# A state-space scan with an MLP behind it: another order of transfers and first steps in the opening

## The chip, the cores and the metric

The kernel runs on one core of a Trainium2 chip. The metric is the device time of one execution in microseconds (us), as the median of the runs shown. Five engines work side by side, each through its own instructions in order: PE (TensorE, the matrix products), VectorE (DVE), ScalarE (ACT), GpSimd (POOL) and SyncE (SP). DMA transfers are issued here from two queues, SP's and ACT's. Tiles in SBUF hold operands, banks of PSUM hold the results of products.

## The reference

Two blocks, one behind the other. The first is a Mamba-2 style scan over 4 batches and 8 heads of 768 positions, with heads of 32 and a state of 16; the second is an MLP with a hard swish over the 3072 resulting rows of 256.

```python
log_a = np.log(np.clip(a, 1e-06, 1.0))
for c in range(nc):                                   # chunks along the sequence
    cum = np.cumsum(la, axis=-1)
    L = np.exp(cum[:, :, :, None] - cum[:, :, None, :]) * causal
    M = np.einsum('bhin,bhjn->bhij', Cc, Bc) * L
    y_intra = np.einsum('bhij,bhjd->bhid', M, xc)
    y_inter = np.einsum('bhin,bhnd->bhid', Cc, state) * np.exp(cum)[:, :, :, None]
    y[:, :, sl] = y_intra + y_inter
    state = decay_full * state + sum_j(B_j x_j * decay_from_j)
h = y_rows @ w_in                                     # (3072, 256) @ (256, 2048)
g = h * np.clip(h + 3.0, 0.0, 6.0) / 6.0
out = g @ w_out                                       # (3072, 2048) @ (2048, 256)
```

Activations are float32; the weights come as 64-bit floats, read as pairs of 32-bit words.

## The kernel before, in words

The sequence is cut into 6 chunks of 128 positions (the kernel's `c` and `k`), each with two halves of 64. A chunk of all 4 batches gives 512 rows for the MLP. While PE multiplies chunk k's MLP, the other engines prepare the scan of the chunk behind it. The program order is written out by hand: each engine runs its instructions in the order in which the code names them, so a waiting instruction holds up what is behind it on its engine. Transfers wait in the same way on the queue that issues them.

**Inputs of chunk 0.** `a` (96 KB), B (`tokens_first`, 256 KB in runs of 64 bytes), C (`pairs_first`, eight transfers of 32 KB, one for each batch and parity of head, in runs of 256 bytes), x (512 KB in runs of 128 bytes), and the weights, eight pieces of 1 MB (`load_w`, rows of 4 KB for `w_in` and 2 KB for `w_out`), of which three fit into SBUF at a time (`raw`). Pieces 0 to 3 are `w_in`, 4 to 7 `w_out`.

**Decoding a piece of weights** (`decode(i)`, advanced by `weights(i, n)` in n steps). 1: ACT copies the upper 16 bits (L198); for piece 0 VectorE also builds the significand (L201, L205). 2: VectorE takes exponent and sign (L215, L217), and L201 for the other pieces. 3: ACT, L221. 4: ACT, L223, with VectorE's L205 for the other pieces; then the piece three further on is loaded. 5: VectorE, L228 and L236, which writes the finished float32 weights to `w_in[i]` or `w_out`.

**The scan of chunk 0.** VectorE clips and adds up log a (L264, L269) and splits the sums (`in_three`); PE forms differences in four banks f0 to f3 (`diff`), ACT their exponentials L (`diff_exp`, L365), and `first_eto` the decay from the chunk's start (L376). `turn_b` turns B on PE (L422) and copies it on ACT (L431). `turn_squares` transposes C on VectorE (L465) and `part_heads` splits it by head parity (L475). `scores` multiplies C and B on PE (L530); `into_state` multiplies B, faded by POOL (`ends`, L396), with x (L544). `multiply` has ACT copy the states (`take` L560, `mid` L569) and VectorE multiply the scores into L (L574). `mix` multiplies that with x (L600) and the state with C (`from_state`, L503); `keep` copies the result to `yT` on ACT (L614). `renew` (L583, L554) forms the next state on VectorE. Also there: `add_up` of the later chunks' sums with `store_rows`, two transfers to DRAM (L286, L288), `turn_cum` (four transposes on PE, L316) with `by_token` (L319), differences and exponentials of chunk 1, and `busy(n, bank)`, n products of the identity with itself that nobody reads (L493).

**The MLP of chunk 0.** 16 groups of products `mlp_in` (L622) over the four banks f0 to f3, each followed by `ramp` on ACT (L726) and `times_ramp` on VectorE (L731), which frees the bank; the decoding of pieces 2 to 5 is woven in between. Group f needs `w_in[f // 4]`. Then `first_out` (L744) multiplies with `w_out`, the first quarter of it first.

The order of the opening ends with the first weights' fifth step, `turn_cum`, chunk 1's share of decoding (piece 1), `mix(0)`, `keep(0)`, and transfers for chunk 1.

Of the kernel before, what the change touches and what calls it, by code (L numbers as in the profile page):

```python
# [8 lines left out]
FP32 = mybir.dt.float32  # L9
# [12 lines left out]
def kernel(  # L22
# [24 lines left out]
    nc = tc.nc  # L47
    P = 128
    NB, NH, S, D = x.shape
    N = B.shape[-1]  # L50
    DM, DF = moe_w_in.shape[0], moe_w_out.shape[0]
    NC = S // P
# [23 lines left out]
    G = NB * NH  # L76
# [9 lines left out]
    def load_bc(c):  # L86

        sl = slice(c * P, (c + 1) * P)  # L90

        def tokens_first(src, queue=nc.sync, **where):
            t = loads.tile([P, NB * NH, N], FP32, **where)
            queue.dma_start(out=t, in_=src[:, :, sl, :].rearrange("b h s n -> s (b h) n"))
            return t

        def pairs_first(src):
            t = loads.tile([P, 2, NB, 4, N], FP32, name="pairs", tag="bc")
            for b in range(NB):
                for h in range(2):  # L100
                    nc.sync.dma_start(  # L101
                        out=t[:, h, b].rearrange("s a n -> s (a n)"),
                        in_=src[b, h:NH:2, sl, :].rearrange("h (s a) n -> h s (a n)", a=4))
            return t

        if 0 < c < TURN:
            bcs[c] = [tokens_first(C, name="C", tag="bc")]
        Bs[c] = tokens_first(B, nc.scalar if c == 0 else nc.sync, name="B", bufs=1)
        if c == 0:
            bcs[c] = [pairs_first(C), Bs[c]]  # L110
        elif c < TURN:
            bcs[c].append(Bs[c])
        else:
            bcs[c] = [pairs_first(C), pairs_first(B)]

    def load_x(c):
        sl = slice(c * P, (c + 1) * P)
        xts[c] = loads.tile([P, NB * NH, D], FP32, name="xt", bufs=1)
        nc.sync.dma_start(out=xts[c], in_=x[:, :, sl, :].rearrange("b h s d -> s (b h) d"))
# [5 lines left out]
    NRAW = 3  # L125
    raws = {}

    def load_w(i, queue=nc.sync):

        raw = loads.tile([P, NK * FP * 2 * P], U32, name="raw", bufs=NRAW)  # L130
        if i < NP:
            cols = slice(2 * i * FP * P, 2 * (i + 1) * FP * P)
            src = moe_w_in[:, cols].rearrange("(k p) f -> p k f", p=P)
            dst = raw.rearrange("p (k f) -> p k f", k=NK)
        else:
            r0 = (i - NP) * FP * P
            src = moe_w_out[r0:r0 + FP * P, :].rearrange("(k p) m -> p k m", p=P)
            dst = raw.rearrange("p (k m) -> p k m", k=FP)
        queue.dma_start(out=dst, in_=src)
        raws[i] = raw  # L140

    load_w(0, nc.scalar)
    load_bc(0)
    load_x(0)
    load_w(1)
    nc.scalar.preload_act_table_set("natural_log_exp_and_others")


# [119 lines left out]
    def add_up(sl):  # L268
        nc.vector.tensor_tensor_scan(  # L269
            out=cum[:, sl], data0=run.rearrange("g c p -> g (c p)")[:, sl], data1=a_sb[:, sl],  # L270
            initial=0.0, op0=ALU.mult, op1=ALU.add)
# [13 lines left out]
    def store_rows():  # L285
        nc.sync.dma_start(  # L286
            out=cum_e[1:].rearrange("c g p -> g c p"), in_=cum_c[:, 1:])
        nc.sync.dma_start(  # L288
            out=cum_d[2:].rearrange("c a g i -> g (c a) i"),
            in_=cum[:, 2 * P:].rearrange("g (k i) -> g k i", i=HT))  # L290
# [23 lines left out]
    def turn_cum(c_ps):  # L314
        for c in range(2, NC):
            nc.tensor.transpose(out=c_ps[:, c], in_=cum_c[:, c], identity=ident[:G, :G])  # L316
# [45 lines left out]
    def diff_exp(c, b):  # L362
        if c not in Ls:
            new_decays(c)
        nc.scalar.activation(Ls[c][:, b], ds.pop((c, b)), AF.Exp)  # L365

    def first_eto():

        e_ps = ps.tile([P, NB, HT], FP32, name="e_ps", tag="f0")
        for b in range(NB):  # L370
            nc.tensor.matmul(
                out=e_ps[:, b],
                lhsT=picks[:, b * P:(b + 1) * P],
                rhs=split[:, 0, HALF[1]], start=(b == 0), stop=True, skip_group_check=True)
        etos[0] = att.tile([P, NB, P], FP32, name="eto")
        nc.scalar.activation(etos[0][:, :, HALF[1]], e_ps, AF.Exp)  # L376
# [30 lines left out]
    def turned(c):  # L407
        if c not in bTs:
            bTs[c] = [att.tile([P, NB, P], FP32, name="bT", bufs=1),
                      att.tile([P, NB, 2, P], FP32, name="cT", bufs=1),  # L410
                      att.tile([P, NB, P], FP32, name="csT", bufs=1)]
        return bTs[c]
# [14 lines left out]
    def turn_b(c):  # L427

        t_ps = turn_ps(c, 1)
        transposes(c, 1, t_ps)  # L430
        nc.scalar.copy(out=turned(c)[0], in_=t_ps)  # L431
# [31 lines left out]
    def turn_squares(t, out):  # L463

        nc.vector.transpose(  # L465
            out=out.rearrange("r b (s a) -> r b a s", a=4),
            in_=t.rearrange("s t b a n -> s (b a) t n"))

    def part_heads(c):
        _, cT, csT = turned(c)  # L470
        for t in range(2):
            if c == TURN:
                nc.scalar.activation(cT[:, :, t], csT, AF.Copy, scale=parity[:, t:t + 1])
            else:
                nc.vector.tensor_scalar(  # L475
                    out=cT[:, :, t], in0=csT, scalar1=parity[:, t:t + 1], scalar2=None,
                    op0=ALU.mult)

    def fade(c, sl=slice(0, P), engine=nc.vector):
        csT = turned(c)[2][:, :, sl]  # L480
        engine.tensor_tensor(out=csT, in0=csT, in1=etos[c][:, :, sl], op=ALU.mult)
# [8 lines left out]
    def busy(n, bank):  # L490

        for _ in range(n):
            nc.tensor.matmul(  # L493
                out=bank.rearrange("p (b i) -> p b i", b=NB), lhsT=ident,
                rhs=ident.unsqueeze(1).to_broadcast([P, NB, P]), start=True, stop=True)
# [20 lines left out]
    def scores(c):  # L516

        bT, cT, _ = bTs[c]
        cbs[c] = [ps.tile([P, NB, 2, HT], FP32, name="cb", tag=f"f{q}") for q in range(NQ)]
        if c not in ys:
            own_banks(c)
        for b in range(NB):
            for a, rows in enumerate(HALF):
                for q in range(NQ):
                    pair = slice(32 * q, 32 * q + 32)
                    nc.tensor.matmul(  # L530
                        out=cbs[c][q][rows, b], lhsT=bT[pair, b, rows],
                        rhs=cT[pair, b, :, rows], start=(b == 0), stop=True,
                        tile_position=(32 * q, a * HT), skip_group_check=True)
        if c == TURN:
            from_state(c, 0)
        into_state(c, *range(2 if c < NC - 1 else 1))

    def into_state(c, *halves):
        xt, bs = xts[c], bss[c]
        for b in range(NB):  # L540
            for q in range(NQ):
                hs = slice(b * NH + 2 * q, b * NH + 2 * q + 2)
                for a in halves:
                    nc.tensor.matmul(  # L544
                        out=sps[c][a][32 * q:32 * q + 32, b],
                        lhsT=bs[HALF[a], hs].rearrange("s h n -> s (h n)"),
                        rhs=xt[HALF[a], hs].rearrange("s h d -> s (h d)"),
                        start=(c == 0 and b == 0), stop=True, tile_position=(a * HT, 32 * q),
                        skip_group_check=True)
# [409 lines left out]
    def weights(i, n):  # L959
        for _ in range(n):  # L960
            next(parts[i], None)


    def diff(c, *bs):
        for part in (diff_less, diff_pick):
            for b in bs:
                part(c, b)
# [10 lines left out]
        mask_again(0, b)  # L978
    diff(0, 0, 1)
    diff(0, 2, 3)  # L980
    weights(0, 1)
    for b in range(NB):
        diff_exp(0, b)
    first_eto()
    diff(1, 2, 3)
    weights(0, 1)
    for b in range(NB):
        ends(0, b)
    turn_b(0)
    diff(1, 0, 1)  # L990
    weights(0, 1)
    diff_exp(1, 2)
    diff_exp(1, 3)
    turn_squares(bcs[0][0], turned(0)[2])
    part_heads(0)
    fade(0, HALF[1], nc.gpsimd)
    add_up(ends_at[1])
    store_rows()
    load_w(2)
    weights(0, 1)  # L1000
    busy(2, ps.tile([P, NB * P], FP32, name="d", tag="f3"))
    scores(0)
    multiply(0)
    load_w(3)
    c_ps = ps.tile([P, NC, G], FP32, name="c_ps", tag="f1")
    turn_cum(c_ps)
    busy(1, ps.tile([P, NB * P], FP32, name="d", tag="f0"))
    weights(0, 1)
    weights(1, 1)
    by_token(c_ps)  # L1010
    mix(0)
    keep(0)
    weights(1, 3)
    renew(0)
    weights(1, 1)
    load_eto(1)
# [153 lines left out]
```

## Time and profile before

| what | value |
|---|---|
| median of 3 runs | 344.35 us (343.89 to 344.46) |
| the profiled execution | 343.51 us |
| its span, first to last instruction | 341.8 us |
| mean granted TensorE clock | 0.999 |
| PE busy | 333.8 us (98%), 3372 instructions |
| VectorE, ACT, POOL busy | 211.9, 188.3, 145.2 us |
| DMA | 25.15 MB, mean 74 GB/s |

Lines of the profile read so: start and length in us, the engine, the line of the kernel, the operation, the tile written `<-` the tiles read, the shapes, and `xN` for N instructions merged. A `q` behind an engine's name (SPq, ACTq) is its queue, where it waits or issues. In brackets stands the time for which the engine was idle before, and what released it. PEld is PE's loading of weights, which runs beside its products. All instants below are us from the start of the span. The packet records of the trace give start, size and queue of every DMA packet.

### The profile page before, as it was taken

The page shows a single profiled execution, that of the slowest core. Times are in us where ns is not written, and L with a number is a line of the kernel's source. Part 1 is how long each engine was busy: PE and PEld are TensorE (multiplying, and loading weights), DVE is VectorE, ACT ScalarE, POOL GpSimd, SP SyncE. Part 2 cuts the span into 40 slices and gives each one's busy share as a digit, 9 for nine tenths or more (in the row PEclk, how much of TensorE's full clock was granted, in tenths as well). Part 3 has the DMA queues.
Part 4 walks back from the last instruction along what each step waited for, and adds up shares of the span by engine and source line. Part 5 has one row for each costly group of instructions (what it writes and reads, how often), then busy time and mean ns, then how long its engine had stood idle before and what let it go on. Part 6 is the DMA issues. An engine that isn't in the chain of part 4 may idle for free.

```text
span 341.8 us, 8204 instructions
## 1 busy us (share of the span) xinstructions
PE 333.8 (98%) x3372; PEld 267.3 (78%) x3372; DVE 211.9 (62%) x332; ACT 188.3 (55%) x394; POOL 145.2 (42%) x139
## 2 busy tenths in 40 slices
PE   6899999999999999999999999999999999999996
PEld 2554458888878888888888888888888888888996
DVE  6599999996599839665519465528465323465011
ACT  4678878667986481675471676470676030576000
POOL 3300000380282898099803099810089500079600
PEclk9999999999999999999999999999999999999999
DMA  8999967052690225167116294001250001110000
GB/s 173 170 312 190 208 245 151 2 61 68 161 117 6 60 62 112 25 83 69 26 40 131 34 99 60 14 4 16 33 74 2 2 2 19 30 17 2 0 33 31
DMA packets 89605, 25.15 MB, mean 74 GB/s; under 512 B 82208, under 2 KB 85952, under 8 KB 89056
## 3 DMA queue, kind: packets, MB, share of 16 engines
q1 hardware_dynamic: 85184, 23.33, 36.9%
q10 hardware_dynamic: 4384, 1.31, 1.8%
q8 instruction: 26, 0.43, 0.5%
q14 instruction: 11, 0.09, 0.1%
HBM read 21.33 MB, written 3.29 MB: 72 GB/s over the span
## 4 chain that ended last, share of the span: by engine, by line
PE 94%; DMA 3%; DVE 1%; SPq 0%; issue 0%; DVEq 0%
PE h L688 33%; PE wb L870 13%; PE wc L870 8%; PE o L744 8%; PE h L622 8%; PE wa L870 8%; PE oa L806 4%; PE ob L806 4%; PE y L600 3%; PE y L503 2%; PE cb L530 2%; DMA raw<-in_moe_w_in_dram 2%; DMA pairs<-in_C_dram 1%; PE y L544 1%; SPq L101 0%; DVE L L574 0%
## 5 line engine op out<-in xcount | busy, mean ns | idle before, releaser
L731 DVE SCALAR_TENSOR_TENSOR gT<-gT,h 128x512 f32<-128x512 f32 x96 | 64.9, 685 | 41.1 <-ACT gT L726 39.9
L726 ACT ACTIVATE gT<-h,half 128x512 f32<-128x512 f32 x96 | 65.1, 684 | 17.8 <-PE h L688 15.9
L792 POOL TENSOR_TENSOR s<-gT 128x512 f32<-128x512 f32 x20 | 28.5, 1425 | 76.2 <-DVE gT L731 76.2
L707 ACT ACTIVATE h<-h 128x512 f32<-128x512 f32 x62 | 35.8, 583 | 43.4 <-PE h L688 37.0
L688 PE MATMUL h<-y_hi,w_part 128*128 128x512 f32 x160 | 51.7, 408 | 0.0
L688 PE MATMUL h<-y_less,w_part 128*128 128x512 f32 x160 | 49.8, 397 | 0.0
L688 PE MATMUL h<-y_lo,w_part 128*128 128x512 f32 x160 | 49.5, 395 | 0.0
L688 PEld LDWEIGHTS h<-y_lo,w_part 128*128 128x128 f32 x160 | 30.0, 188 | 7.4
L688 PEld LDWEIGHTS h<-y_less,w_part 128*128 128x128 f32 x160 | 30.0, 188 | 6.8
L688 PEld LDWEIGHTS h<-y_hi,w_part 128*128 128x128 f32 x160 | 30.0, 188 | 6.6
L385 ACT ACTIVATE L<-L,cum_n 128x64 f32<-128x64 f32 x128 | 31.5, 336 | 0.0
L870 PE MATMUL wb<-s,w_out 128*128 128x256 f32 x128 | 30.7, 382 | 0.0
L744 PE MATMUL o<-w_out,gT 128*128 128x256 f32 x128 | 28.8, 381 | 0.0
L622 PE MATMUL h<-yT,w_in 128*128 128x512 f32 x64 | 27.7, 594 | 0.0
L744 PEld LDWEIGHTS o<-w_out,gT 128*128 128x128 f32 x128 | 24.1, 190 | 3.8 <-issue 0.5
L403 POOL TENSOR_TENSOR tmp<-state,eto 128x256 f32<-128x256 f32 x5 | 3.3, 669 | 55.2 <-ACT eto L389 55.1
L870 PEld LDWEIGHTS wb<-s,w_out 128*128 128x128 f32 x128 | 24.0, 190 | 3.6
L792 POOL TENSOR_TENSOR s<-gT,s 128x512 f32<-128x512 f32 x20 | 25.9, 1300 | 1.3
L792 POOL TENSOR_TENSOR gT<-gT 128x512 f32<-128x512 f32 x20 | 25.6, 1288 | 1.3
L792 POOL TENSOR_TENSOR s<-s,gT 128x512 f32<-128x512 f32 x20 | 25.6, 1287 | 0.0
L158 POOL TENSOR_SCALAR_AFFINE_SELECT L<-L 64x1024 f32<-64x1024 f32 (+1 forms) x16 | 20.9, 1310 | 10.7 <-PE h L688 5.3
L622 PEld LDWEIGHTS h<-yT,w_in 128*128 128x128 f32 x64 | 12.1, 190 | 14.9 <-issue 13.2
(138 smaller groups left out, 509.0 us busy)
## 6 DMA issues: line engine op xcount, KB each, us to landing
raw<-in_moe_w_out_dram SPq DMA_DIRECT2D x4, 1024.0 KB
L<-cum_d SPq DMA_DIRECT2D x8, 512.0 KB
xt<-in_x_dram SPq DMA_DIRECT2D x6, 512.0 KB
raw<-in_moe_w_in_dram SPq DMA_DIRECT2D x3, 1024.0 KB
out_dram<-back SPq DMA_DIRECT2D x128, 16.0 KB
pairs<-in_C_dram SPq DMA_DIRECT2D x40, 32.0 KB
eto<-cum_e SPq DMA_DIRECT2D x20, 64.0 KB
B<-in_B_dram SPq DMA_DIRECT2D x5, 256.0 KB
```

Of the source, the lines that this page charges most:

```text
L158: nc.gpsimd.affine_select(out=t[rows], in_=t[rows], pattern=pattern, compare_op=ALU.is_ge, fill=-1e5, base=base, channel_multiplier=-1)
L385: nc.scalar.activation(Ls[c][:, b, h], Ls[c][:, b, h], AF.Exp, bias=cum_n[:, c, g:g + 1])
L600: nc.tensor.matmul(out=ys[c][a, u][d0:d0 + D, b], lhsT=xt[rows, b * NH + h], rhs=Ls[c][rows, b, h], start=(b == 0 and a >= min(c, 1)), sto ...
L622: nc.tensor.matmul(out=h, lhsT=w_in[f // FP][:, j, f % FP * P:(f % FP + 1) * P], rhs=yTs[k][:, j].rearrange("p b i -> p (b i)"), start=(j ...
L688: nc.tensor.matmul(out=hs_[k, f], lhsT=w[j][:, f % FP * P:(f % FP + 1) * P], rhs=y[:, j], start=(start and j == 0), stop=True, skip_group_ ...
L707: nc.scalar.activation(h, h, AF.Copy, scale=1.0 / EPS + 1.0)
L726: nc.scalar.activation(gTs[k][:, f], h, AF.Relu, bias=half, scale=1.0 / 6.0)
L731: nc.vector.scalar_tensor_tensor(out=g, in0=g, scalar=1.0, in1=h, op0=ALU.min, op1=ALU.mult)
L744: nc.tensor.matmul(out=o[:, b % 2], lhsT=gTs[0][:, f, b * P:(b + 1) * P], rhs=w_out[:, f], start=(f == 0 and b % 2 == 0), stop=True, skip_ ...
L792: nc.gpsimd.tensor_tensor(out=o, in0=p_, in1=q_, op=op)
L806: nc.tensor.matmul(out=bank[:, slot], lhsT=lhs[:, j], rhs=rhs[:, j], start=(clear and j == 0), stop=True, skip_group_check=True)
L870: nc.tensor.matmul(out=bank[:, slot], lhsT=lhs[:, j], rhs=rhs[:, j], start=(clear and j == 0), stop=True, skip_group_check=True)
```

## The change

- Transfers: the first weights go from ACT's queue to SP's, behind C and ahead of x. Of C's eight transfers two (batch 0 and batch 1, even heads) go on ACT's queue; B follows them there.
- The second weights' transfer is no longer issued at the start. `load_w(1, held=True)` writes one column of its tile by a VectorE memset, and the transfer waits for that. The memset stands behind VectorE's second step of the first weights and ahead of `multiply(0)`.
- Order: C's transposition, head split, the later chunks' sums and their stores come ahead of the first weights' decoding and of most of the exponentials; `turn_b` comes ahead of chunk 1's first differences. The first weights' steps 3 and 4 stand ahead of `scores(0)`. `into_state(0)` is called on its own, behind chunk 1's second pair of differences. `mix(0)` comes ahead of `turn_cum`, `by_token` and `keep(0)`, and the second weights' decoding starts behind `keep(0)`.
- Both calls of `busy` are gone.

```diff
             for b in range(NB):
                 for h in range(2):
-                    nc.sync.dma_start(
+                    queue = nc.scalar if c == 0 and (b, h) in ((0, 0), (1, 0)) else nc.sync
+                    if c == 0 and (b, h) == (1, 1):
+                        Bs[0] = tokens_first(B, nc.scalar, name="B", bufs=1)
+                    queue.dma_start(
...
-        Bs[c] = tokens_first(B, nc.scalar if c == 0 else nc.sync, name="B", bufs=1)
         if c == 0:
-            bcs[c] = [pairs_first(C), Bs[c]]
-        elif c < TURN:
+            t = pairs_first(C)
+            bcs[c] = [t, Bs[c]]
+            return
+        Bs[c] = tokens_first(B, name="B", bufs=1)
+        if c < TURN:
...
-    def load_w(i, queue=nc.sync):
+    def load_w(i, held=False):
         raw = loads.tile([P, NK * FP * 2 * P], U32, name="raw", bufs=NRAW)
+        if held:
+            nc.vector.memset(raw[:, 0:1], 0)
...
-        queue.dma_start(out=dst, in_=src)
+        nc.sync.dma_start(out=dst, in_=src)
...
-    load_w(0, nc.scalar)
     load_bc(0)
+    load_w(0)
     load_x(0)
-    load_w(1)
...
-        into_state(c, *range(2 if c < NC - 1 else 1))
+        if c:
+            into_state(c, *range(2 if c < NC - 1 else 1))
...
     diff(0, 0, 1)
     diff(0, 2, 3)
+    turn_squares(bcs[0][0], turned(0)[2])
+    part_heads(0)
+    add_up(ends_at[1])
+    store_rows()
+    diff_exp(0, 0)
+    diff_exp(0, 1)
+    first_eto()
+    diff_exp(0, 2)
+    diff_exp(0, 3)
+    turn_b(0)
     weights(0, 1)
-    for b in range(NB):
-        diff_exp(0, b)
-    first_eto()
     diff(1, 2, 3)
-    weights(0, 1)
     for b in range(NB):
         ends(0, b)
-    turn_b(0)
-    diff(1, 0, 1)
+    fade(0, HALF[1], nc.gpsimd)
     weights(0, 1)
     diff_exp(1, 2)
     diff_exp(1, 3)
-    turn_squares(bcs[0][0], turned(0)[2])
-    part_heads(0)
-    fade(0, HALF[1], nc.gpsimd)
-    add_up(ends_at[1])
-    store_rows()
+    weights(0, 2)
+    scores(0)
+    load_w(1, held=True)
+    diff(1, 0, 1)
+    into_state(0, 0, 1)
+    multiply(0)
     load_w(2)
     weights(0, 1)
-    busy(2, ps.tile([P, NB * P], FP32, name="d", tag="f3"))
-    scores(0)
-    multiply(0)
+    mix(0)
+    c_ps = ps.tile([P, NC, G], FP32, name="c_ps", tag="f2")
+    turn_cum(c_ps)
+    by_token(c_ps)
+    keep(0)
     load_w(3)
-    c_ps = ps.tile([P, NC, G], FP32, name="c_ps", tag="f1")
-    turn_cum(c_ps)
-    busy(1, ps.tile([P, NB * P], FP32, name="d", tag="f0"))
-    weights(0, 1)
-    weights(1, 1)
-    by_token(c_ps)
-    mix(0)
-    keep(0)
-    weights(1, 3)
+    weights(1, 4)
     renew(0)
     weights(1, 1)
     load_eto(1)
```

## The prediction

> **What bounds the kernel now.** I read the page first, part 4 (the chain that ended last, as shares of the span).
>
> ```profile
> PE 94%; DMA 3%; DVE 1%; SPq 0%; issue 0%; DVEq 0%
> ```
>
> PE carries 94%, so the rest lies in the opening. Next the chain in order of time (start, length, what):
>
> ```profile
> 0.80 6.15 DMA raw<-in_moe_w_in_dram
> ...
> 8.65 4.13 DMA pairs<-in_C_dram
> ...
> 12.96 1.25 DVE csT L465
> 14.23 0.89 DVE cT L475 x2
> 15.26 1.25 PE cb L530 x60
> 16.51 1.30 DVE L L574 x2
> 18.29 1.05 PE d L493 x2
> ...
> 22.56 27.66 PE h L622 x64
> 50.23 13.81 PE o L744 x64
> ```
>
> C's landing starts VectorE's transposition (L465) at 12.96; chunk 0's last product ends at 22.56; from there PE runs without a hole. The timeline of SP and ACT shows why C is late: the first weights (1 MB) go ahead of it.
>
> ```profile
> 0.80 0.47 ACTq L139 DMA_DIRECT2D raw<-in_moe_w_in_dram  x1
> 1.26 8.06 SPq L101 DMA_DIRECT2D pairs<-in_C_dram  x8
> 9.37 0.94 SPq L119 DMA_DIRECT2D xt<-in_x_dram  x1
> 10.36 3.56 SPq L139 DMA_DIRECT2D raw<-in_moe_w_in_dram  x1
> ```
>
> Last, the question that decides: can PE's stage after 22.56 use an earlier start? The busy time by stage (us, then PE, PEld, DVE, ACT, POOL) and VectorE's timeline there:
>
> ```profile
> 27.10:36.00 8.90, 8.90 (x22) 3.90 (x21) 8.66 (x15) 6.94 (x10) 0.00 (x0) 1.00 1.03 148
> 43.20:50.10 6.90, 6.90 (x18) 3.08 (x17) 6.70 (x11) 5.64 (x7) 0.00 (x0) 1.00 0.59 222
> ```
> ```profile
> 20.97 0.42 DVE L215 TENSOR_SCALAR we<-ws 128x1024 uint16<-128x1024 uint16 x1
> 27.11 1.28 DVE L731 SCALAR_TENSOR_TENSOR gT<-gT,h 128x512 f32<-128x512 f32 x2
> 41.07 1.23 DVE L236 SCALAR_TENSOR_TENSOR w_in<-wm,we 128x1024 f32<-128x1024 f32 x1
> 48.07 1.23 DVE L236 SCALAR_TENSOR_TENSOR w_out<-wm,we 128x1024 f32<-128x1024 f32 x1
> ```
>
> VectorE is 97% busy there. It finishes w_in's last quarter at 42.30 for products that start at 43.2, and w_out's first quarter at 49.30 for products that start at 50.06. The tighter slack is 0.76, 0.70 after 0.06 from a VectorE end to PE (as 7.09 to 7.15, L280 to L348). So PE gains at most 0.70 plus what VectorE's own sequence gains.
>
> **When C arrives.** The trace's packet records (start, size and queue of each packet) say that each C transfer posts 4 completion writes where B, x and weights post 16: it runs on four of sixteen DMA engines. C and B together lay on the four from 5.24 to 11.84; beside B a C transfer took 1.0, alone 0.45. With the first weights behind C, packets start 1.0 to 1.3 after the first issue (a: 0.80 to 1.82, weights: 0.80 to 2.09), at 1.9. ACT issues two C transfers and then B (0.6 to 0.7 each, as C's issues on SP), so B starts at 3.4: three C transfers alone are 1.4, five beside B 5.0, the end is 8.3. From C's last packet to L465 it was 1.1 (11.84 to 12.96), so **S = 9.4** in place of 12.96. Bounds: 7.9, if only SP's issues pace it (last of six at 5.0, 1.3 to its packets, 0.45, 1.1), and 10. I take 9.4, because all of C and B shared those engines in the rows.
>
> ACT's extra issues push the table load's end from 3.10 to about 4.05; L266, 3.96 now, slips by 0.1. VectorE's chain behind it ended at 7.09, so 2.2 of cover hides that until S.
>
> **From S to chunk 0's end.** VectorE's order is now L465, L475, L269 (12.96 to 16.23: 3.27), then the first weights' L201 and L205 (7.12 to 8.99: 1.87): L215 starts at S + 5.14. L215 to ACT's L221 is 0.46 (35.31 to 35.77), L221 to L223 1.18 (22.88 to 24.06), to ACT's next 1.06 (24.06 to 25.12). These now stand on ACT ahead of chunk 0's adds and mid: 0.90 (17.28 to 18.18). Then 0.05, and PE's from_state, mix, from_state: 0.61 + 0.80 + 0.61 by the chain. The sum is S + 10.8: **T = 20.2** in place of 22.56. The idle products cost the chain 1.05 at 18.29; that is part of the difference. The multiplies L574 start at S + 6.1 = 15.5; two (1.3) are done by 16.8, and mix's first half by 17.7, before mid at 18.15.
>
> Covers: the first weights, issued at about 5.8 by SP after its C transfers, need 6.15 as now (0.80 to 6.95): 11.95, against L201 at 12.67; beyond 0.7 it would count in full. x is last of a, C, B, first weights and x; this same set ended at 15.10 before, and the four engines start as early, so I put it there again, plus 0.9: into_state at 16.0 and mid 1.8 later, 17.8 against 18.15 (cover 0.3; bounds of x's landing 15.2 to 16.6). B, landed by 9, gives a bT copy at 9.8 and is covered. The stores of the sums move from 16.26 to 12.7 on SP, ahead of the held transfer: nothing. The four turn_cum transposes (0.43) now stand between mix and h on PE, and VectorE's L319 waits for them in a hole: hidden in the stall below.
>
> **The second weights.** Their decoding moves. ACT's copy (L198) ran at 18.77, ahead of chunk 0's yT copies; now it runs after them, at T + 0.32 (22.56 to 22.88) = 20.5. And the transfer waits for the memset (0.06), behind L217: S + 6.0 = 15.4. SP stands there, with weights 2 to 4 and chunk 1's loads behind it; chunk 1's are first used at 64, so that is covered. How long an unhindered 1 MB takes is not shown: 6.15 from issue to use for the first weights; as lower end 4.3 (1.0 to the first packet, 256 packets of 4 KB at the fastest rate seen, 101 a us from 16.5 to 17.5, and 0.77 of landing, 6.18 to 6.95). I take 5.2, between them, since x will be through: 20.6. So L198 runs at **W = 20.6**, the later of both.
>
> VectorE: L198 to L215 1.15; L215 to the end of L554 3.73 (20.97 to 24.70); L228 to L731 1.87 (25.24 to 27.11): 6.75, at 27.35 instead of 27.11. So VectorE's sequence is 0.25 *later* although chunk 0 ends 2.4 earlier: what is removed ahead of 22.56 returns as PE waiting at the fifth product group (its bank is freed by L731) and at the quarters of weights. Gain: 0.70 - 0.25 = **0.45**; break-even is W = 21.05. The profiled execution took 343.51 (span 341.8, 1.7 around it), so it would take 343.05; the median of the runs, 344.35, is 0.84 above it, and the prediction on that scale is 343.9.
>
> Removed idle products: PE's longest new hole, between chunk 1's differences (over by 14.3) and into_state at 16.0, is 1.7. In the rows the eight masks at 2.13 took 3.57 (0.45 each), the same 512 columns at 7.15 0.30: PE starts at half speed and then keeps full speed through holes of up to 0.9. The Trainium skill, "TensorE: Matmul & The Clock Gate", Part 1, says that PE falls back to half clock after an idle window of about 3.4 us; by it the new hole would not do it, and no run here shows a hole so long.
>
> **Rivals.**
> - *C comes sooner* (faster): S = 7.9. Then x (16.0) sets the end: T = 19.9, W = 20.2, gain 0.85 (L201 starts at 11.95 with the first weights, the held transfer gives 19.9). With x at 15.2 and both weight transfers at the lower end W is 19.4, gain 1.65. I take 1.1: **343.2**. For: four C transfers are issued before B has packets. Against: 1.0 each beside B.
> - *The held transfer sets the pace* (slower). The same transfer took 8.4 in the trace (issue 10.36 to L198 at 18.77), behind x. If x's tail or the later weights stretch it to 7.2, half way from 6.15, then W = 22.6 and the loss is 1.55: **345.9**. It decides from 5.65 after the memset on. For: x may still be moving at 15.4, on the same queue. Against: the next 1 MB flowed at the full rate.
> - *B is caught behind the first weights.* C's first packet, on another queue, waited for the first weights (5.62, as these ended at 6.18). If a rest of B waits for them in the same way on the four engines, B lands at 12.2; bT copy, ACT's row of copies and Relus and the tail are 8.6: T = 20.8, W = 21.15, gain 0: **344.4**. The Trainium skill, "DMA: Bandwidth & Descriptors", Queues, rings and completion order, has each engine alternate between queues by whole packets of several descriptors; the row of C's wait agrees.
> - *C no earlier, or PE at half speed.* If C kept landing at 12.8, T = 23.8 and the loss is 3; one window of 3.4 at half speed costs 1.7, of which some 0.8 hides in the stall.
>
> **How the numbers follow.** A measurement of this kernel can tell about 0.2%, 0.7 us. Chances: forecast 0.38, of which 0.10 (W below 20.35) is a gain over 0.7; C sooner 0.28; held transfer 0.22; B caught 0.04; the last 0.08. Faster 0.28 + 0.10 = 0.38; same 0.28 + 0.04 = 0.32; slower 0.22 + 0.08 = 0.30. Low end 342.9 (C sooner, x near its lower bound); high end 345.9, the held transfer's price.
>
> **What would show it.** Right: L465 at about 9.4; L201 right behind L269; the last chunk 0 product at about 20.2; L198's second run at 20.6; L731 first at 27.3; PE holes of about 1 us at the fifth product group and more before w_out's products, which start at 49.6. Wrong: holes ahead of L201 (first weights late), of into_state (x), of L198 (second weights), or no PE holes in the h stage, which would make the gain over 2.

## The result, and the profile after

The change made the kernel slower: 348.19 us (median of 20 runs, 345.68 to 348.94) against 344.31 for the kernel before (20 runs beside them, 343.26 to 347.77), a ratio of 1.010 [1.008, 1.0119]. The forecast was 343.9 with a range of 342.9 to 345.9; the time lies outside it. Ratios here and below leave out runs more than 1.5% above a kernel's shortest run, so with few runs they can stand off the ratio of the medians. The profiled execution took 347.24 (span 345.5).

The page of after first: the row of granted clock over 40 slices of 8.6 us, and the chain that ended last by engine.

```profile
PEclk9989999999999999999999999999999999999999
...
PE 83%; DVE 8%; ACT 4%; DMA 2%; SPq 1%; issue 1%; DVEq 0%
```

Two things differ from before. The third slice (17 to 26) has a granted clock of 0.8, where before had 9 in every slice. And PE, which carried 94% of the chain, carries 83%: VectorE's 8% and ACT's 4% are now on it. The chain in order of time (start, length, what) says where:

```profile
4.65 5.39 DMA pairs<-in_C_dram
...
10.12 1.14 DVE csT L471
...
12.32 1.13 DVE pre L275
13.45 0.60 DVE wm L207
14.07 1.64 DVE wm L211
15.71 0.35 DVE we L221
16.08 1.16 ACT we L227
17.26 1.15 ACT we L229
18.41 0.27 ACT adds L567
18.68 0.04 issue
18.72 1.14 PE y L607 x64
...
22.78 0.37 ACT yT L621
23.16 1.03 ACT ws L204
24.21 0.44 DVE we L221
24.67 1.16 ACT we L227
25.85 1.16 ACT we L229
```

(The change shifts these places of the code by 6 or 7 lines: the L198, L201, L205, L215, L221, L223, L465, L600, L614, L731 and L744 of the prediction are L204, L207, L211, L221, L227, L229, L471, L607, L621, L738 and L751.) C's transposition starts at 10.12 in place of 12.96, so C is 2.8 sooner. All of it is gone when chunk 0's last product ends: 22.73, where it was 22.56. PE's timeline shows the two reasons:

```profile
15.53 0.85 PE L551 MATMUL y<-xt,bs 64*32 64x64 f32 x64 [0.70 <-DMA xt<-in_x_dram]
18.72 1.14 PE L607 MATMUL y<-L,xt 64*32 64x64 f32 x64 [2.34 <-ACT adds L567]
19.79 1.11 PE L509 MATMUL y<-csT,mid 32*64 32x64 f32 x16
20.83 1.18 PE L607 MATMUL y<-L,xt 64*32 64x64 f32 x64
21.95 0.79 PE L509 MATMUL y<-csT,mid 32*64 32x64 f32 x16
```

First, `mix` does not start when its factors are there: PE idles 2.34 until ACT's copy of the states, `adds`, has ended, since that copy reads the PSUM bank into which `mix` writes. Second, the four groups of products behind the hole take 1.14, 1.11, 1.18 and 0.79; the last one's 0.79 falls into full speed again. The trace's clock records put half speed from 18.81 to 22.22, one window of 3.41. Behind it ACT starts the second weights, and from there on VectorE sets the time:

```profile
23.05 1.12 ACT L204 COPY ws<-raw 128x1024 uint16<-128x1024 uint16 x1
```
```profile
29.72 1.28 DVE L738 SCALAR_TENSOR_TENSOR gT<-gT,h 128x512 f32<-128x512 f32 x2
```

These answer to 18.77 (L198) and 27.11 (L731) before. The first products with `w_out` start at 52.07 in place of 50.06: 2.0 of the profile's 3.7. The other 1.7 came at two later places: 87 to 105, where one VectorE operation took 1.47 in place of 0.68, and at 118, where PE's hole of 0.43 was 1.13. Of kernels with nearly the same instants in the opening (g4 and f1 below) the span grew by no more than 0.4 beyond what `w_out` lost. The longer operation is not explained; the hole at 118 comes again in other kernels without the idle products (see "What stays open" below), so it is not only this execution's.

The one profile shows the mildest case of the clock. Of the 20 runs of after, four had a granted clock of 1.000 (345.68, 346.23, 346.30, 346.79). The other sixteen had 0.984 to 0.995, and eleven of them 0.984 or 0.985: 1.5% of 347 is 5.2 us of full-speed clock, or 10.4 at half speed, three windows of 3.41. For before's 20 runs the record has no clock; of the 92 runs of before that stand beside the experiments below, 87 had 0.998 or more and five had 0.994 or 0.995.

### The profile page after: what moved, and what is told of

The parts are those of the page before. It is cut to its first block, busy times and chain, and to the rows that moved or that the text cites. A ratio compares the mean times of both kernels' runs of the same rounds, so it can differ in the third digit from the quotient of the medians.

```text
span 345.5 us, 8195 instructions
## 1 busy us (share of the span) xinstructions
PE 332.5 (96%) x3366; PEld 266.6 (77%) x3366; DVE 213.7 (62%) x333; ACT 187.6 (54%) x394; POOL 146.5 (42%) x139
## 4 chain that ended last, share of the span: by engine, by line
PE 83%; DVE 8%; ACT 4%; DMA 2%; SPq 1%; issue 1%; DVEq 0%
PE h L695 29%; PE wb L877 12%; PE wc L877 8%; PE o L751 8%; PE wa L877 8%; PE oa L813 4%; PE ob L813 4%; PE y L607 3%; DVE gT L738 2%; PE y L509 2%; PE h L629 2%; DMA pairs<-in_C_dram 2%; PE cb L536 2%; ACT we L227 1%; PE y L551 1%; DVE wm L211 1%
## 5 line engine op out<-in xcount | busy, mean ns | idle before, releaser
L738 DVE SCALAR_TENSOR_TENSOR gT<-gT,h 128x512 f32<-128x512 f32 x96 | 64.9, 686 | 41.2 <-ACT gT L733 39.9
L629 PE MATMUL h<-yT,w_in 128*128 128x512 f32 x64 | 28.4, 599 | 0.7 <-DVE w_in L242 0.4
L751 PE MATMUL o<-w_out,gT 128*128 128x256 f32 x128 | 28.9, 381 | 0.0
L751 PEld LDWEIGHTS o<-w_out,gT 128*128 128x128 f32 x128 | 24.0, 190 | 4.1 <-ACT gT L733 0.8
```

The lines of the kernel that those rows point to most:

```text
L629: nc.tensor.matmul(out=h, lhsT=w_in[f // FP][:, j, f % FP * P:(f % FP + 1) * P], rhs=yTs[k][:, j].rearrange("p b i -> p (b i)"), start=(j ...
L738: nc.vector.scalar_tensor_tensor(out=g, in0=g, scalar=1.0, in1=h, op0=ALU.min, op1=ALU.mult)
L751: nc.tensor.matmul(out=o[:, b % 2], lhsT=gTs[0][:, f, b * P:(b + 1) * P], rhs=w_out[:, f], start=(f == 0 and b % 2 == 0), stop=True, skip_ ...
```

## The experiments

Two theories stood at the start. **Clock**: without the idle products PE's activity in the hole ahead of `mix` is so low that the clock falls, and that is most of the loss. **VectorE's sequence** (the expectations call it placement): the second weights' decoding starts later (at W, the start of ACT's L204 for them), VectorE's chain to the first L738 is 6.7 long, and PE waits for it, whatever its clock. A third came up with the first results: **the fetch of PE's instructions**, a transfer that can be caught behind the weights.

### The idle products put back, and taken out alone

e1 is the changed kernel with both calls; e2 is the kernel before without them.

```diff
+    busy(2, ps.tile([P, NB * P], FP32, name="d", tag="f3"))
     scores(0)
...
+    busy(1, ps.tile([P, NB * P], FP32, name="d", tag="f0"))
     mix(0)
```

> The changed kernel with the idle products put back: two ahead of scores, one ahead of mix. Clock theory (PE's hole between into_state and mix lets the clock fall to half, so mix takes 4.0 in place of 2.9): granted clock 0.999 in every run, mix and from_state done by 21.7 in place of 22.7, the second weights' first step (ACT, L204) about 1.0 earlier, the runs close together at about 346.3, which is where the runs of the changed kernel with clock 1.000 lie. Placement theory (the second weights' decoding stands behind chunk 0's end): what is left over the kernel before is then about 2 us, all of it from L204 starting at about 22 in place of 18.8. If the clock were the whole loss, the time would be 344.3 or less.

> The kernel before without its idle products, nothing else. Clock theory: part of the runs show a granted clock of 0.985 to 0.995 and are 0.5 to 2 us longer. Placement theory: the second weights' first step stays at 18.8, ahead of mix, so without a fall of the clock the time stays at 344.3, although mix starts up to 1 us sooner, since VectorE has only 0.7 to give.

e1: 344.73 (12 runs), ratio 1.0019 [1.0004, 1.0034], clock 0.999 or more in all 12. e2: 348.32 (6 runs), ratio 1.0123 [1.009, 1.0155], clock 0.976 to 0.995 in all 6. So the idle products are worth 3.5 us between the medians of after and e1 (2.8 by the two ratios, 1.0100 and 1.0019), and 3.9 between e2 and the runs of before beside it (344.41). In e2's profile the clock fell 0.7 behind the end of a hole of only 1.37, ahead of the first `from_state`, and stayed down for 6.83.

```profile
20.75 0.68 PE L503 MATMUL y<-csT,mid 32*64 32x64 f32 x16 [1.37 <-ACT yT L614]
```

The releaser that this line names cannot be the right one: `keep`'s copy to `yT` comes behind `from_state` in the program's order, and it had ended at 20.46. PE was waiting for its instructions, as shown under "The transfer held back, or not". So taking the idle products out did not make chunk 0 shorter in e2: `from_state` starts at 20.75, where it was 20.48. PE's timeline of e1, and then the windows (stretch and length; busy time of PE, PEld, VectorE, ACT, POOL; granted clock, DMA share, GB/s), of after and of e1:

```profile
17.48 1.13 PE L499 MATMUL d<-ident 128*128 128x512 f32 x2 [0.93 <-DVE L L581]
19.03 0.86 PE L607 MATMUL y<-L,xt 64*32 64x64 f32 x64 [0.43 <-ACT adds L567]
19.82 0.68 PE L509 MATMUL y<-csT,mid 32*64 32x64 f32 x16
```
```profile
15.00:19.00 4.00, 1.13 (x89) 1.00 (x97) 3.97 (x9) 3.06 (x6) 0.00 (x0) 0.98 0.43 97
19.00:23.00 4.00, 4.00 (x163) 3.46 (x144) 1.73 (x2) 1.53 (x5) 0.00 (x0) 0.60 0.91 335
```
```profile
15.00:19.00 4.00, 2.67 (x99) 1.58 (x98) 3.96 (x8) 2.65 (x5) 0.00 (x0) 1.00 0.36 81
19.00:23.00 4.00, 3.97 (x166) 3.28 (x167) 2.33 (x4) 2.68 (x7) 0.00 (x0) 1.00 0.98 402
```

With the products in the hole PE is busy 2.67 of 4.0 in place of 1.13, the clock stays at 1.00, and the group of 64 products takes 0.86 in place of 1.14. What is left in e1 is the rest of the change: its W is 22.21, its first L738 28.87 and `w_out` starts at 51.20, 1.14 later than before. That is VectorE's theory in its own kernel. Between these two profiled executions it is worth 1.26 us, between the medians 0.3 (0.2%), where about 2 us were expected.

### Which of the idle products

f1 has only the round ahead of `mix`, g4 only the two ahead of `scores`; each diff is against e1.

```diff
-    busy(2, ps.tile([P, NB * P], FP32, name="d", tag="f3"))
     scores(0)
```
```diff
-    busy(1, ps.tile([P, NB * P], FP32, name="d", tag="f0"))
     mix(0)
```

> The changed kernel with only the idle product ahead of mix put back (1.1 us of PE), not the two ahead of scores. Clock theory, if it is the hole of 2.3 us between into_state and mix that counts: clock 1.000 in nearly every run and the time of the run with all idle products, 344.7, or less. If the busy share of the whole stretch from the first differences on counts, half the runs still fall: 346 to 347 in the median, clock 0.985 to 0.995.

> The changed kernel with only the two idle products ahead of scores, not the one ahead of mix. If the hole of 2.3 us between into_state and mix is what lets the clock fall, it still falls: 0.985 to 0.995 in most runs, 347 to 348.5. If the total of idle work since the first differences counts, the clock stays: 344.7 to 345.5.

f1: 345.28 (12), ratio 1.0032 [1.0013, 1.0051], clock 0.998 or more in 12 of 12. g4: 345.99 (12), ratio 1.005 [1.0031, 1.007], clock 0.985 to 0.990 in 10 of 12. One round of idle products in the right place does what two elsewhere do not; g4's hole and its slow groups are those of after:

```profile
18.67 0.91 PE L607 MATMUL y<-L,xt 64*32 64x64 f32 x64 [2.12 <-ACT adds L567]
19.51 1.11 PE L509 MATMUL y<-csT,mid 32*64 32x64 f32 x16
```

f1's clock held, and yet it shows a second cost of the change on ACT, with the idle time ahead of it in brackets:

```profile
23.41 1.12 ACT L204 COPY ws<-raw 128x1024 uint16<-128x1024 uint16 x1 [1.39 <-DMA raw<-in_moe_w_in_dram]
```

Here the held transfer took 6.9 from its memset (16.48) to its use, where e1 needed no more than 5.45, and the first L738 came at 30.08. It is the prediction's second rival. It comes in one more profile, of h1 below: there ACT waits 2.02 for the transfer, which took 7.6, and the first L738 comes at 30.66.

### Time at work, or part of the array at work

g1 puts many small products (64x32 of the array, 64 columns) in place of the whole ones. h1 and h2 are f1 with the one call narrowed: the same two instructions of 512 columns, on 64x32 or on 128x32 of the array.

```diff
-    busy(1, ps.tile([P, NB * P], FP32, name="d", tag="f0"))
+    narrow(1, ps.tile([P, NB * P], FP32, name="d", tag="f0"))
...
+            nc.tensor.matmul(
+                out=bank[:32].rearrange("p (b i) -> p b i", b=NB), lhsT=ident[:64, :32],
+                rhs=ident[:64].unsqueeze(1).to_broadcast([64, NB, P]), start=True, stop=True,
+                tile_position=(0, 0))
```

> The changed kernel with idle products put back in both places, but as tiles of 64 rows by 32 columns like mix's own (72 of them ahead of scores, 48 ahead of mix) in place of whole 128x128 ones. If the clock follows the time for which PE has any product in work, it stays full as with the whole products: 1.000, 344.7. If it follows how much of the array works, the small ones count for little and the clock falls as without any: 0.985 to 0.995, 347 to 348.5.

> The changed kernel with one idle product ahead of mix, as in the run with one whole product (two instructions, 1.1 us of PE, 512 columns), but with a tile of 64 rows by 32 columns of the array in place of 128 by 128: the same time and the same number of instructions, an eighth of the array. If the clock follows the time for which PE works: 1.000 in nearly every run, 345.3 as with the whole product. If it follows how much of the array works: 0.985 to 0.995 in most runs, 347 to 348.5.

> The same with 128 rows by 32 columns, a quarter of the array. Time theory: 1.000 and 345.3. Array theory: between the two, the clock falls in a part of the runs, 346 to 348.

g1: 357.11 (4), ratio 1.0367 [1.0349, 1.0385], clock 0.975 to 0.980. It does not answer the question: with its 120 more products PE ran out of instructions for 4.71 us in the midst of them (see the next part), a hole that no theory of the clock had asked for. h1: 346.1 (12), ratio 1.0041 [1.0016, 1.0066], clock 0.980 to 0.990 in 6 of 12. h2: 344.77 (12), ratio 1.0011 [0.9991, 1.0031], clock 1.000 in 12 of 12. PE's timelines of h1 and of h2:

```profile
17.15 1.04 PE L506 MATMUL d<-ident 64*32 64x512 f32 x2 [0.48 <-DVE L L589]
```
```profile
17.37 1.04 PE L506 MATMUL d<-ident 128*32 128x512 f32 x2 [0.74 <-DVE L L589]
```

Same count, same 1.04 us, same place; with 64 rows of the array the clock fell in half the runs, with 128 in none. So the clock does not go by PE's time alone. The number of columns (128 in f1, 32 in h2) made no difference here.

The clock records let all profiles answer the same question. They change only at multiples of 3.41 after the first full speed, so each profile can be cut into stretches of 3.41 that end where the clock could have fallen. For each stretch at full speed take the share of time for which PE has a product at work, and count each instant by the rows in use (64 of 128 count half). The 16 profiles have 1544 such stretches. The eight at whose end the clock fell have shares of 0.27 or less (g1 0.00, e3 0.12, after 0.14, g2 0.15, e4 0.16, g4 0.19, e2 0.21, f4 0.27). Of all others one stretch of e2 is as low (0.21), and the next has 0.29. Plain time, without the rows, does not divide them: f4's clock fell behind a stretch with 0.73 and held behind one with 0.57. This is one profile per kernel, and the ends of products are modelled, so the limit itself is only bracketed.

### The transfer held back, or not

e3 is the changed kernel with the second weights' transfer at the start, behind x, and no memset; f4 is the same edit made to e1, with the idle products.

```diff
     load_x(0)
+    load_w(1)
...
     scores(0)
-    load_w(1, held=True)
```

> The changed kernel with the second weights' transfer not held: it is issued behind x at the start. Placement theory: L204's second run waits for chunk 0's end and not for the transfer, so the time is that of the changed kernel (347.5 to 348.5 in the median, within 0.3 us of it). Held-transfer theory: L204 moves to 21 or sooner and the time falls by 1.5 us or more.

> The changed kernel with the idle products back and the second weights not held. Placement theory: L204's second run still waits for chunk 0's end, so the time stays at 344.7 within 0.3. Held-transfer theory: the transfer lands sooner and L204 moves ahead by up to 1 us, 344.0 or less. If the hold keeps x or the first weights free of other traffic, as the change in words suggests, into_state or L204's first run come later here and the time rises by up to 1 us.

e3: 349.38 (5), ratio 1.0155 [1.0134, 1.0177]. f4: 348.24 (6), ratio 1.011 [1.0077, 1.0144], clock 0.985 to 0.994 in all 6. Without the hold both are slower than with it, e1 to f4 by 3.5. PE's timelines of e3 and of f4 show a kind of hole that after and e1 lack:

```profile
21.53 1.00 PE L510 MATMUL y<-csT,mid 32*64 32x64 f32 x13 [1.18 <-issue]
```
```profile
18.89 0.82 PE L608 MATMUL y<-L,xt 64*32 64x64 f32 x61 [0.44 <-ACT adds L568]
21.15 0.30 PE L608 MATMUL y<-L,xt 64*32 64x64 f32 x3 [1.43 <-issue]
```

"issue" is time for which the profile has no releaser, here in the middle of a row of equal products. The packet records have a packet of 16 KB on an instruction queue near each such hole:

| kernel | second weights' first packet | instruction packet: start, length | PE resumes at | hole |
|---|---|---|---|---|
| e3 | 14.86 | 19.15, 0.95 | 21.53 | 1.18 |
| f4 | 14.70 | 18.71, 0.95 | 21.15 | 1.43 |
| f2 (below) | 14.51 | 18.64, 0.96 | 20.96 | 0.89 |
| g2 (below) | 16.96 | 20.81, 1.04 | 23.06 | 3.18 |
| g1 | 17.78 | 21.87, 1.01 | 24.23 | 4.71 |
| e2 | 14.85 | 18.35, 0.98 | 20.75 | 1.37 |
| e4 (below) | 14.44 | 18.72, 0.96 | 21.20 | 1.75 |
| before | 14.57 | 17.89, 1.01 | 20.24 | under 0.1 |
| after | 17.59 | 17.06, 0.94 | | none |
| e1 | 17.96 | 16.66, 1.13 | | none |

Where the weights' 256 packets come first, the instruction packet starts 3.3 to 4.3 behind the first of them, near their end, and PE goes on 1.2 to 1.5 after its end. Where it comes first, PE has no such hole. Only the place of the weights' transfer differs between after and e3 and between e1 and f4, and in both the packet comes 2.1 later. That is what the hold is good for, whatever it costs in the weights' arrival: it lets the instructions through. In the kernel before, the packet is late as well, but the idle products fill the time, and PE arrives when the instructions do. How much of the 3.5 is the hole itself and how much the fall of the clock behind it, these runs do not divide.

No record names the packets' engine, but a count does. In seven of the eight profiles of the table in which PE resumes, its first record (product, load of weights or other) behind the hole has exactly 705 ahead of it. In the eighth, g1, PE has three such holes, at 17.66, 24.23 and 28.88, with 705, 961 and 1217 records ahead, steps of 256. The Trainium skill, "Runtime: NRT & Kernel Launch", Instruction fetch mechanics, says that each engine's instruction memory is refilled in blocks of 16 KiB, 256 instructions, over a DMA queue and that this is mostly hidden; the packets' size and the steps agree, and these holes are where it is not hidden.

### The second weights decoded sooner

e4 is e3 with the old order of the decoding: `turn_cum`, `by_token` and the second weights' first step ahead of `mix`. f2 is e4 with the idle products.

```diff
-    weights(0, 1)
-    mix(0)
-    c_ps = ps.tile([P, NC, G], FP32, name="c_ps", tag="f2")
+    c_ps = ps.tile([P, NC, G], FP32, name="c_ps", tag="f1")
     turn_cum(c_ps)
+    weights(0, 1)
+    weights(1, 1)
     by_token(c_ps)
+    mix(0)
     keep(0)
     load_w(3)
-    weights(1, 4)
+    weights(1, 3)
```

> As the one before (not held), and with the order of the kernel before behind the multiplies: turn_cum, the first weights' last step, the second weights' first step and by_token ahead of mix. No idle products. Placement theory: L204's second run at about 19.2, VectorE's first L738 at about 27.3 in place of 29.7, PE's first w_out product at about 50.2 in place of 52.1, the time 344.5 in runs with a clock of 1.000 and up to 346 in others. Clock theory alone: no gain over the changed kernel, since the hole ahead of mix is as long as before.

> The second weights not held and their first step ahead of mix, as in the run of that order, now with the idle products back. With the clock held full that run's other half is seen. Placement theory: L204's second run at about 19, the first L738 at about 26.4 in place of 28.9, the first w_out product at 49.4, 0.7 before that of the kernel before: 343.7, ratio 0.998. If placement does not matter: 344.7, as with the idle products alone.

e4: 349.39 (5), ratio 1.0137 [1.0114, 1.0159], clock 0.990 or less in 5 of 5. Its W is 18.96, 4.1 sooner than in after, yet its `w_out` starts at 53.18, 1.1 later than in after (1.4 sooner than in e3), since PE stands still for 1.75 ahead of the first `from_state`:

```profile
21.20 1.12 PE L510 MATMUL y<-csT,mid 32*64 32x64 f32 x16 [1.75 <-ACT yT L622]
```

As in e2, the `yT` copy that is named here comes later in the program's order and had ended, at 20.37; what PE waits for is the instruction packet of the table.

f2: 347.92 (6), ratio 1.0124 [1.0087, 1.0161]. Two of its runs kept the clock (343.94, 344.23), four lost it (347.52 to 349.53). Its profile is of the run of 344.23, and even that has the hole of the table: chunk 0 ends at 23.28, and `w_out` starts at 50.78, 27.50 behind it, as in the kernel before. So PE and not VectorE sets the start of `w_out` there, and sooner decoding bought nothing.

### ACT's step ahead of the states, and an earlier release

f3 is e1 with the first weights' step 4 (L229, 1.15 on ACT) moved behind `multiply`, so that `adds` and `mid` need not wait for it. g2 is f3 with the hold released one step sooner. g3 is the kernel before with one move of its own: chunk 0's second weights' step 2 and 3 stand ahead of the third yT copy.

```diff
-    weights(0, 2)
+    weights(0, 1)
     busy(2, ps.tile([P, NB * P], FP32, name="d", tag="f3"))
...
-    weights(0, 1)
+    weights(0, 2)
     busy(1, ps.tile([P, NB * P], FP32, name="d", tag="f0"))
```
```diff
     fade(0, HALF[1], nc.gpsimd)
+    load_w(1, held=True)
     weights(0, 1)
...
     scores(0)
-    load_w(1, held=True)
```
```diff
         for a, u in ((0, 0), (0, 1), (1, 0), (1, 1)) if c else ((0, 0), (1, 0), (0, 1), (1, 1)):
+            if c == 0 and (a, u) == (0, 1):
+                weights(1, 2)
...
-    weights(1, 3)
+    weights(1, 1)
```

> The changed kernel with the idle products back, and the first weights' fourth step (ACT, L229, 1.15 us) moved from ahead of scores to behind chunk 0's adds and mid. If mix waits for adds (ACT reads the bank that mix writes), adds starts at about 17.4 in place of 18.6 and mix follows the idle product at 18.6 in place of 19.0: 0.4 us, 344.3. If mix waits for something else, nothing moves: 344.7.

> The kernel with idle products and the late Relu, and the held transfer released one step sooner, behind L211 in place of L223: the memset at about 15.8 in place of 16.6, the transfer landed at 21.4 in place of 22.2. If the second weights' landing is what sets L204 there (22.20, with chunk 0's end at 21.39), L204 starts at 21.7, the first L738 at 28.35, the first w_out product at 50.7 (L738 plus 22.33): 0.5 less, 344.9 against the 345.4 of that kernel in the median. If PE's instruction fetch (16.7) is caught behind the sooner weights, PE stands still in mix for up to 1.4 and the time rises to 346 or more.

> The kernel before, with one move: the second weights' second and third steps (VectorE, and ACT's L221 by that kernel's numbering) stand between chunk 0's second and third yT copies in place of behind the fourth. VectorE theory: L221 at about 21.6 in place of 22.9, L223 23.0, VectorE's hole of 0.54 ahead of L228 closes, the first L731 at 26.6 in place of 27.1, the first w_out product 0.5 sooner (49.5), the time 343.8, ratio 0.9985. PE theory (chunk 0's end bounds): the two late yT copies delay the first h products by 0.4 to 0.8 and the time stays or rises to 345.

f3: 345.43 (12), ratio 1.0035 [1.0015, 1.0056], clock 0.998 or more throughout. `mix` starts at 18.41 and chunk 0 ends at 21.39, 0.6 and 0.5 sooner than in e1, as expected; but ACT then waits 0.39 for the held transfer and starts the second weights at 22.20, as in e1 (22.21). The gain stops there, and the time, expected at 344.3, is not shorter than e1's.

g2: 345.81 (12), in two groups: six runs at 343.87 to 344.52 with a clock of 0.999 or more, six at 347.1 to 350.45 with 0.990 to 0.995; its ratio, 1.001 [0.9988, 1.0032], rests on the first group and one run of the second. PE's timeline of a run of the second group:

```profile
23.06 0.30 PE L607 MATMUL y<-L,xt 64*32 64x64 f32 x3 [3.18 <-issue]
```

One step sooner is enough for the weights' packets to be ahead of the instructions in that run. It also started late: its clock came to full speed at 10.73, in f3's profile at 5.02, and the instruction packet ahead of this one started at 13.92 in place of 11.18. Whether all six runs of the group began so is not shown. The first group is as short as before, no shorter.

g3: 343.85 (12), ratio 0.9987 [0.9975, 1.0000], the shortest median of all, though its interval touches 1. Its first L731 is 0.72 sooner than before, at 26.39, and `w_out` still starts at 50.11: the expected gain at that point did not come.

## Why the prediction was wrong

**What VectorE's sequence does** was right in form. In every profile in which VectorE sets the pace, `w_out`'s first product starts 22.3 after the first L738: after 29.72 and 52.07, e1 28.87 and 51.20, f1 30.08 and 52.41, f3 28.85 and 51.19, g4 29.75 and 52.27 (22.52). PE's own bound is chunk 0's end plus 27.5 (22.56 and 50.06 before; 22.61 and 50.11 in g3, which explains g3's miss: there PE, not VectorE, was the bound). Before, L731 plus 22.33 gave 49.44, a slack of 0.62 where the prediction read 0.70. Its sum for a given W held too: W to the first L738 is 6.66 in e1 and 6.67 in after, 6.75 forecast.

**The steps to W were too early.** In e1, where the clock stays out of it, S is 10.23 (9.4 forecast, upper bound 10), the memset S + 6.5 (S + 6.0), chunk 0's end 21.90, S + 11.7 (S + 10.8), and W 22.21 (20.6). The term in S was mis-sized by 0.8: two C transfers took ACT 1.73 to issue, B's last packet started at 8.46, and C's last at 9.19 (forecast for the end: 8.3). Of the 0.9 behind it in e1, 0.5 is VectorE's L207, which took 1.20 in place of 0.69, and 0.3 is the first half of `mix`, which runs behind `adds` and not ahead of `mid`. In after it is L211 that grew. Its row and POOL's, from after's timelines:

```profile
14.07 1.64 DVE L211 SCALAR_TENSOR_TENSOR wm<-raw,wm 128x1024 f32<-128x1024 uint32 x1
```
```profile
12.40 2.23 POOL L487 TENSOR_TENSOR csT<-csT,eto 128x256 f32<-128x256 f32 x1 [0.36 <-DVE cT L481]
```

L211 takes 1.23 elsewhere in the same profile (25.73), and L487 took 1.50 before; here, where the change puts them side by side, they take 1.64 and 2.23. In e1 L487 takes 1.62 and L211 1.22. That the two engines hold each other up is inferred from these rows; no run took them apart. With W at 22.21 the prediction's own rule, break-even at 21.05, gives a loss of 1.16; e1's `w_out` lost 1.14.

**The hole ahead of `mix`** is a smaller step that failed. The text had the first half of `mix` done by 17.7, before `mid`; it did not see that `mix` writes the bank which ACT's `adds` still reads. With L227 and L229 ahead of `adds` on ACT, PE's longest hole was 2.34 and not 1.7, and it came later, between small products. The prediction also took the idle products' 1.05 on the chain as time to be gained; e2 shows that without them PE waits for its instructions instead.

**The clock term** is the step that failed most, and that took the time out of the range: removing the idle products was put at no cost, since the new hole was taken to be too short to matter. "PE at half speed" stood among the rivals with part of a chance of 0.08 and a price of 1.7 for one window, 0.8 of it hidden. Measured, it came in 16 of 20 runs, mostly for three windows, and cost 2.8 to 3.5 in the median; e2 shows it in the kernel before by the removal of the idle products alone. With the clock held, in e1, the change takes 344.73: inside the range, though a little slower and not faster. In after, g4 and e2 holes of 2.34, 2.12 and 1.37 were enough. The prediction went by the idle window of about 3.4 us that the Trainium skill, "TensorE: Matmul & The Clock Gate", Part 1, states; these holes were shorter. The Trainium skill has a second passage in "TensorE: Matmul & The Clock Gate", A second HAM failure mode: psum-queue depth-cycling, where frequent short idle times between groups of products make the clock swing. It was not weighed. It is nearer to these runs in that short idle times were enough, but after shows only two holes there (0.70 and 2.34), so it is no full match.

**Right in small things**: L207 directly behind L275, into_state released by x (15.5, 16.0 forecast), and PE holes at the fifth product group (0.30) and ahead of the last quarter of `w_in` (0.37). That the first weights were in time for L207 was luck: ACT waited for them until 13.04, 1.1 later than the 11.95 of the forecast, and S was late by 0.7 as well. **The held transfer** took 5.45 or less in e1 (5.2 forecast) but 6.9 in f1 and 7.6 in h1 (the rival's 7.2): it is level with chunk 0's end, and nothing that ends chunk 0 sooner would have gained from there.

**What stays open.** The four full-clock runs of after have a mean of 346.25, 1.5 above e1's median, though `mix` starts no later than in e1; no profile shows after at full clock. A part is seen in the hole at 118. PE's timelines of after and of before:

```profile
119.17 0.33 PE L551 MATMUL y<-xt,bs 64*32 64x64 f32 x11 [1.13 <-issue]
```
```profile
115.53 0.35 PE L544 MATMUL y<-xt,bs 64*32 64x64 f32 x16 [0.43 <-issue]
```

Both have 2497 of PE's records ahead of them (705 and seven times 256), and in after PE goes on 1.3 behind the end of an instruction packet (117.85). In the profiles of the four kernels with neither call of `busy` (after, e2, e3, e4) this hole is 0.97 to 1.21, in the others, g1 aside, 0.65 or less. Without the calls PE has six products and six loads of weights fewer, so the same count falls at another place of the order. Against e1's 0.53 that would be 0.6 of the 1.5; the rest is open. Nor was it measured why the fall lasts one window in some runs and three in others.

## What to carry to other kernels

An instruction that computes nothing can be holding the clock: before idle products go, look at PE's busy share in their stretch without them (1.13 of 4.0 lost the clock in most runs, 2.67 of 4.0 kept it), weighted by the rows of the array that are at work, and price a fall by several windows, in the median of many runs, not in one profile. When a step is moved, check which PSUM bank the products behind it write and which engine still reads it: here ACT's decoding steps, put ahead of that read, opened PE's hole. Ask of every large transfer what may be caught behind it: here holding it back made ACT wait for it in some runs (1.39 in f1, 2.02 in h1) and paid that back by letting PE's instructions pass. And where the releaser that a line names had ended long before, or comes later in the program, look for another: here it was the fetch of instructions.

## What the runs showed of the hardware

- The clock fell at holes of 1.4 to 2.3 us between small products (e2, g4, after), not only in a long idle time. In all profiles it fell behind stretches of 3.41 in which PE's time at work, counted by rows in use, was 0.27 or less. In the records of the opening half speed lasts whole multiples of 3.41 (3.41 in after and f4, 6.83 in e2 and g4, 10.24 in e3, 13.65 in g1), and the same kernel loses it in some runs only: 16 of 20 in after, 10 of 12 in g4, 6 of 12 in h1, 5 of 92 in before. The Trainium skill, "TensorE: Matmul & The Clock Gate", Part 1, has the window at 3413 ns and free-running, so that its phase differs from run to run; the records agree with both (full speed first comes at 5.02 in f3 and at 11.23 in e2).
- The rows of the array at work count for it: 1.04 us of products on 128 rows kept the clock in 12 of 12 runs, the same time on 64 rows in 6 of 12.
- A packet of PE's instructions waits behind weights that were issued first: it starts 3.3 to 4.3 us behind their first packet in the table above, and 2.1 later than where it comes first. PE goes on 1.2 to 1.5 after the packet's end, and stood still for up to 3.2 us (4.7 in g1, with more instructions).
